# Loading the last 768 columns of one weight block as eight transfers of 21, 18, 10 and 1 rows

## The chip, the cores and the metric

The kernel runs on one core of one Trainium2 chip. The metric is device time in microseconds of that core, as the median of several executions. Most executions of one kernel agree within 0.3%; the trace holds the start, duration and size of every DMA packet and the moments at which the DMA engines that carry a transfer report their shares as landed. Neither record names the engine.

## The reference, cut to what matters

One token passes through grouped-query attention over a cache of 65536 keys and values in 4 groups, and beside it through a gated mixer. The two results are mixed with a gate. Only the last product of the attention half matters here:

```python
o = jnp.einsum('bhqk,bhkd->bhqd', p, v)
return o.transpose(0, 2, 1, 3).reshape(B, Sq, Hq * Dh) @ wo      # wo: 4096 x 1024, bf16, 8.4 MB
...
return g * a + (1 - g) * b
```

Everything is read once: 162 MB from HBM. So the time is that of one long load, with the arithmetic beside it.

## The kernel before

All large loads go through one queue, issued by the SP engine into a ring of buffers in SBUF. The order is fixed: keys and values, then the output weights as four quarters. Each quarter is 1024 rows of the matrix laid on 128 partitions, eight matrix rows (16 KB) a partition. The last quarter is cut in three, so that only a small piece is left for the end.

```python
def load(keys, src, off):
    n = len(stream)
    w = src.shape[1]
    ...
    stream.append((keys, off, src))

def rows(w, i, c):
    return w[128 * c * i:128 * c * (i + 1), :].rearrange("(p c) n -> p (c n)", c=c)
...
WO_AT = [0, 8 * DO, 16 * DO, 24 * DO]
WO_CUT = [(0, 5), (5, 7), (7, 8)]
for i in range(3):
    load([("wo", i, 0)], rows(A_wo, i, 8), WO_AT[i])
for c0, c1 in WO_CUT:
    load([("wo", 3, c0)], rows(A_wo, 3, 8)[:, DO * c0:DO * c1], WO_AT[3] + DO * c0)
...
P("SP", lambda e, o=OFF["RING"] + off, w=w, src=src: e.dma_start(arena[:, o:o + w], src),
  w=[("slot", x) for x in gr], dma="s%d" % gr[0])
```

A helper records each operation with what it reads and writes, and turns these into semaphore waits. It counts 16 on the semaphore for each complete transfer (`dma_count` in the kernel).

## Time and profile before

| | before |
|---|---|
| time, median | 381.83 us (381.75 to 382.3, 4 runs) |
| span in the profile | 380.3 us |
| data moved | 162.17 MB, 426 GB/s over the span |
| PE, DVE busy | 62%, 54% |
| latest landing of the last weights | 378.23 us |

The page has one row per engine or quantity over 40 slices of the span. The row of the transfer rate in the profile of the kernel before:

```profile
GB/s 435 427 420 400 469 388 438 441 469 431 401 414 441 441 443 427 434 410 424 477 441 434 434 434 414 415 441 441 434 407 433 445 441 441 436 403 424 419 426 262
```

Read it as a whole: with the DMA engines 90% busy or more in every slice but the last (the prediction shows that row), the rate stays around 430 GB/s. The prediction shows the other lines, and how the landings of single engines are read.

### The profile page before, as it was taken

Reading aid. Unit: us, or ns where it says so; the run is one execution under the profiler, and the core shown is the slowest. Engines: PE = TensorE matmul, PEld = TensorE weight load, DVE = VectorE, ACT = ScalarE, POOL = GpSimd, SP = SyncE. Lnnn points to the kernel's source line nnn. Section 1 sums busy time; section 2 is a strip of 40 time slices with the busy share of each in tenths; the row PEclk is TensorE's granted clock in tenths of the full one; section 3 lists DMA queues with packets and bytes.
Section 4 is the critical chain, followed back from the end, with each engine's and each line's share of the span. In section 5 each row is a group of like instructions: output and inputs, shape, how many; then the busy total and the mean of one; then the engine's idle time right before and its main releaser. Section 6 shows DMA issues by size and latency. Waiting matters only on the chain.

```text
span 380.3 us, 2581 instructions
## 1 busy us (share of the span) xinstructions
PE 235.1 (62%) x1449; PEld 58.1 (15%) x836; DVE 204.6 (54%) x162; ACT 23.3 (6%) x24; POOL 8.4 (2%) x37
## 2 busy tenths in 40 slices
PE   0061388458558924895788138952895884739378
PEld 0010011011111200122112001220121110212015
DVE  4011496778389525965892249745774882312020
ACT  1000000010420000002200000022000000220000
POOL 5000000000000000000000000000000000000000
PEclk9998599696859985998699859995899697958689
DMA  9999999999999999999999999999999999999996
GB/s 435 427 420 400 469 388 438 441 469 431 401 414 441 441 443 427 434 410 424 477 441 434 434 434 414 415 441 441 434 407 433 445 441 441 436 403 424 419 426 262
DMA packets 4254, 162.17 MB, mean 426 GB/s; under 512 B 532, under 2 KB 532, under 8 KB 788
## 3 DMA queue, kind: packets, MB, share of 16 engines
q1 hardware_dynamic: 4208, 162.01, 98.9%
q8 instruction: 9, 0.15, 0.2%
q10 hardware_dynamic: 36, 0.00, 0.0%
q14 instruction: 1, 0.01, 0.0%
HBM read 162.01 MB, written 0.00 MB: 426 GB/s over the span
## 4 chain that ended last, share of the span: by engine, by line
DMA 56%; PE 23%; DVE 18%; ACT 1%; issue 1%; SPq 0%; ACTq 0%; DVEq 0%
DMA arena<-in_A_k_cache_dram 34%; DVE arena L502 15%; DMA arena<-in_A_wo_dram 10%; DMA arena<-in_A_v_cache_dram 8%; PE scp L260 7%; PE scp L262 6%; DMA arena<-in_B_b_sp_dram 5%; PE obt L260 4%; PE obt L262 4%; DVE arena L539 1%; PE fbt L712 1%; PE fbt L660 1%; ACT arena L534 1%; SPq L389 0%; ACTq L288 0%
## 5 line engine op out<-in xcount | busy, mean ns | idle before, releaser
L502 DVE STREAM_TRANSPOSE arena<-arena 128x2048 f32<-128x2048 f32 x64 | 143.0, 2284 | 48.2 <-DMA arena<-in_A_k_cache_dram 32.7
L260 PE MATMUL scp<-arena 128*128 128x512 bf16 (+1 forms) x275 | 112.8, 429 | 87.7 <-DVE arena L502 86.3
L262 PE MATMUL scp<-arena 128*128 128x512 bf16 (+1 forms) x279 | 113.1, 427 | 0.0
L260 PE MATMUL obt<-arena 128*64 128x512 bf16 (+2 forms) x334 | 62.9, 419 | 17.5 <-DMA arena<-in_A_v_cache_dram 17.5
L262 PE MATMUL obt<-arena 128*64 128x512 bf16 (+2 forms) x334 | 62.2, 414 | 0.0
L260 PEld LDWEIGHTS scp<-arena 128*128 128x128 bf16 (+1 forms) x275 | 27.7, 104 | 200.1 <-issue 101.3
L539 DVE STREAM_TRANSPOSE arena<-arena 128x2048 bf16<-128x2048 bf16 x7 | 16.2, 2311 | 28.5 <-PE obt L262 26.4
L534 ACT ACTIVATE arena<-arena 128x2048 bf16<-128x2048 f32 x8 | 16.0, 2002 | 218.6 <-DVE arena L531 195.6
L260 PEld LDWEIGHTS obt<-arena 128*64 128x64 bf16 (+1 forms) x334 | 18.3, 113 | 70.7 <-issue 56.1
L519 DVE TENSOR_SCALAR_CACHE_REDUCE arena<-scp 128x2048 f32<-128x2048 f32 x8 | 18.3, 2292 | 16.0 <-PE scp L262 16.0
L580 PE MATMUL mbt<-arena 128*128 128x128 bf16 x16 | 1.9, 258 | 12.6 <-DVE arena L575 12.6
L542 DVE STREAM_TRANSPOSE arena<-arena 128x1024 bf16<-128x1024 bf16 x2 | 2.5, 1246 | 12.7 <-PE obt L262 12.7
L490 POOL COPY arena<-arena 32x32 bf16<-32x32 bf16 x16 | 3.2, 203 | 234.5 <-PE scp L262 209.7
L568 DVE RECIPROCAL arena<-mbt 128x1 f32<-128x1 f32 x4 | 0.6, 139 | 14.1 <-PE mbt L563 14.1
L531 DVE TENSOR_REDUCE arena<-mbt 128x1 f32<-128x32 f32 x4 | 0.8, 192 | 13.5 <-PE mbt L528 13.5
L437 PE MATMUL mbt<-arena 1*128 1x2 bf16 x1 | 0.2, 158 | 12.3 <-DMA arena<-in_B_b_sp_dram 12.3
L439 DVE COPY arena<-mbt 128x2 f32<-128x2 f32 x1 | 0.2, 160 | 12.3 <-PE mbt L437 12.3
L775 DVE CAST arena<-fbt 36x128 bf16<-36x128 f32 x1 | 0.3, 283 | 11.0 <-PE fbt L712 11.0
L432 PE MATMUL scp<-arena 8*128 8x1 bf16 x8 | 0.7, 199 | 8.7 <-DVE arena L427 8.7
L712 PE MATMUL fbt<-arena 128*32 128x128 bf16 x128 | 4.1, 220 | 0.1
L712 PEld LDWEIGHTS fbt<-arena 128*32 128x32 bf16 x128 | 3.6, 97 | 1.6 <-DMA arena<-in_A_wo_dram 0.8
L467 DVE CAST arena<-obt 97x1024 bf16<-97x1024 f32 x1 | 1.2, 1225 | 4.9 <-PE obt L262 4.9
(91 smaller groups left out, 54.2 us busy)
## 6 DMA issues: line engine op xcount, KB each, us to landing
arena<-in_A_k_cache_dram SPq DMA_DIRECT2D x6, 4096.0 KB, 33.1
arena<-in_A_v_cache_dram SPq DMA_DIRECT2D x2, 4096.0 KB, 26.0
arena<-in_B_w_in_dram SPq DMA_DIRECT2D x1, 7168.0 KB, 30.4
arena<-in_A_wo_dram SPq DMA_DIRECT2D x3, 2048.0 KB, 33.4
arena<-in_B_w_out_dram SPq DMA_DIRECT2D x1, 3584.0 KB, 21.5
arena<-in_A_wo_dram SPq DMA_DIRECT2D x1, 1280.0 KB, 30.3
arena<-in_A_wo_dram SPq DMA_DIRECT2D x1, 512.0 KB, 31.0
arena<-in_A_wo_dram SPq DMA_DIRECT2D x1, 256.0 KB, 30.8
```

The lines of the kernel that those rows point to most:

```text
L260: return e.matmul(*a, **kw)
L262: one = e.matmul(*a, **kw).ins
L467: P("DVE", lambda e: e.tensor_copy(psb[0:97, :], ob[0:97, :]), w=["psb", "ob"])
L490: P("POOL", lambda e, pb=pb: e.tensor_copy(vw(qpad, 24 + 32 * pb, [[QP, 4], [1, 8]], 32 * pb, 32), vw(qall, 8 * g, [[32, 4], [1, 8]], 32 * ...
L502: P("DVE", lambda e: e.transpose(ktb(i).bitcast(F32), sl[:, 4096 * p:4096 * (p + 1)].bitcast(F32)), r=keys[4 * p:4 * p + 4], w=[("kt", i % ...
L519: P("DVE", lambda e: e.tensor_scalar(scs(j), scp[:, :], 0.0, None, op0=ALU.add, op1=ALU.max, accum_out=maxc[:, j:j + 1]), w=[("sc", j % 2) ...
L534: P("ACT", lambda e: e.activation(psb2, scs(j), ACTF.Exp, bias=gcol(j // 2, K_NB), scale=SCALE, accum_out=lp[:, j:j + 1]), r=[("sc", j % 2 ...
L539: P("DVE", lambda e: e.transpose(ptsb2, psb2), r=["psb"], w=[("ptsb", 0), ("ptsb", 1)])
L542: P("DVE", lambda e: e.transpose(ptsb(n), ab("PSB", 1024, 1024 * (n % 2))), r=["psb"], w=[("ptsb", n % 2)])
L580: ins = e.matmul(mb[:, 0:128], sel[:, 128 * c:128 * (c + 1)], osc[:, 128 * c:128 * (c + 1)], start=(c == 0), stop=(c == 3))
L660: ins = e.matmul(fb[32 * b:32 * (b + 1), 0:QW], e4z[0:97, 31 - j:63 - j], part[0:97, QW * s:QW * (s + 1)], start=(first and s % (NW // 2) ...
L712: ins = e.matmul(fb[32 * b:32 * (b + 1), 0:QW], ovz[:, z:z + 32], sl[:, o:o + QW], start=False, stop=(i == 3 and c == 7), tile_position=(0 ...
```

## The change

Its intent: at the end of the load some DMA engines are done over a microsecond before others (seven of 16 landings of the last weights at 376.57 to 377.06 us, nine at 377.89 to 378.23). So a slice of one block, 768 of 8192 columns of the first quarter, is not shared equally among 16 engines but meant mainly for three of them. Each piece is written in the edit with the number of engines that it is meant for: 3, 9, 10 or 1.

```diff
-    def load(keys, src, off):
+    def load(keys, src, off, cut=None):
...
+        dst = arena[:, OFF["RING"] + off:OFF["RING"] + off + w]
+        parts = [(dst, src)]
+        if cut:
+            c, pieces = cut
+            parts = [(dst[:, 0:w - c], src[:, 0:w - c])]
+            for r0, step, k, h in pieces:
+                o, (row, _) = OFF["RING"] + off + w - c, src.ap[0]
+                parts.append((bass.AP(tensor=arena, offset=r0 * NA + o, ap=[[step * NA, h], [1, c]]),
+                              bass.AP(tensor=src.tensor, offset=src.offset + r0 * row + w - c,
+                                      ap=[[h // k * step * row, k], [step * row, h // k], [1, c]])))
...
+    LOW = [(r, 6, 3, 21) for r in (0, 2, 4)] + [(r, 6, 9, 18) for r in (1, 3, 5)] + [(109, 2, 10, 10), (126, 1, 1, 1)]
...
-        load([("wo", i, 0)], rows(A_wo, i, 8), WO_AT[i])
+        load([("wo", i, 0)], rows(A_wo, i, 8), WO_AT[i], cut=(768, LOW) if i == 0 else None)
...
-            P("SP", lambda e, o=OFF["RING"] + off, w=w, src=src: e.dma_start(arena[:, o:o + w], src),
-              w=[("slot", x) for x in gr], dma="s%d" % gr[0])
+            P("SP", lambda e, todo=todo: [e.dma_start(dst, x) for dst, x in todo],
+              w=[("slot", x) for x in gr], dma="s%d" % gr[0], parts=len(todo))
```

A piece (r0, step, k, h) takes h rows from r0 on, every step-th, and is meant for k engines.

More of the change, by code (lines that the diff above doesn't have):

```diff
@@ L29, in __init__, with op @@
         self.early = 0
-    def op(self, eng, fn, r=(), w=(), dma=None):
+    def op(self, eng, fn, r=(), w=(), dma=None, parts=1):
         o = Op()
@@ L50, in op @@
         if dma is not None:
-            self.dma_count[dma] = self.dma_count.get(dma, 0) + 16
+            self.dma_count[dma] = self.dma_count.get(dma, 0) + 16 * parts
             o.dma = (dma, self.dma_count[dma])
@@ L112, in run @@
                 if o.dma:
-                    last.then_inc(dsem[o.dma[0]], 16)
+                    for x in last if isinstance(last, list) else [last]:
+                        x.then_inc(dsem[o.dma[0]], 16)
                 elif o.inc:
@@ L312, in load @@
             place[key] = (n, off + i * (w // len(keys)), w // len(keys))
-        stream.append((keys, off, src))
+        dst = arena[:, OFF["RING"] + off:OFF["RING"] + off + w]
[8 more added lines that the diff above has]
+                                      ap=[[h // k * step * row, k], [step * row, h // k], [1, c]])))
+        stream.append((keys, off, w, parts))
     def rows(w, i, c):
@@ L379, in issue @@
             n = issued[0]
-            keys, off, src = stream[n]
-            w = src.shape[1]
+            keys, off, w, todo = stream[n]
             gr = grains(off, w)
```

## The prediction

> **What bounds the kernel now.** I read the page first, then busy time by stretches, the chain of waits, and last the timeline of the final microseconds. The page's rows by slice and its queue table say that the transfers fill the whole span:
>
> ```profile
> DMA  9999999999999999999999999999999999999996
> ...
> DMA packets 4254, 162.17 MB, mean 426 GB/s; under 512 B 532, under 2 KB 532, under 8 KB 788
> ...
> q1 hardware_dynamic: 4208, 162.01, 98.9%
> q8 instruction: 9, 0.15, 0.2%
> ```
>
> Every slice but the last is 90% busy or more, while PE is busy 62% of the span and DVE 54%. The stretches (columns: stretch, length, busy time of PE, PEld, DVE, ACT, POOL, then clock, DMA share, GB/s) show that only the first and last pieces have any slack:
>
> ```profile
> 60.00:180.00 120.00, 78.86 (x454) 18.36 (x242) 78.76 (x65) 10.30 (x11) 1.62 (x8) 0.83 1.00 433
> 180.00:300.00 120.00, 79.28 (x405) 17.50 (x208) 76.21 (x46) 6.28 (x6) 0.81 (x4) 0.83 1.01 435
> 360.00:376.50 16.50, 13.87 (x160) 5.23 (x121) 2.58 (x6) 1.02 (x1) 0.00 (x0) 0.84 0.98 414
> 376.50:380.30 3.80, 2.17 (x64) 1.79 (x64) 0.28 (x1) 0.00 (x0) 0.00 (x0) 1.00 0.19 69
> ```
>
> The chain in the last 12 us (start, length, what) goes through the output weights:
>
> ```profile
> 331.05 37.33 DMA arena<-in_A_wo_dram
> ...
> 376.50 1.77 PE fbt L712 x56
> ...
> 378.27 0.42 PE fbt L712 x8
> ```
>
> And the timeline shows the end: the last eight matmuls wait for the last piece of those weights, then a cast, then the store.
>
> ```profile
> 378.27 0.23 PEld L712 LDWEIGHTS fbt<-arena 128*32 128x32 bf16 x8 [0.18 <-DMA arena<-in_A_wo_dram]
> 378.79 0.28 DVE L775 CAST arena<-fbt 36x128 bf16<-36x128 f32 x1 [11.04 <-PE fbt L712]
> 379.10 0.31 SPq L366 DMA_DIRECT2D out_dram<-arena  x1
> ```
>
> The trace's semaphore marks give the 16 landings of that last piece: 376.57, .57, .60, .61, .65, .96, 377.06, then 377.89, .98, 378.03, .03, .12, .17, .18, .22, .23. So **seven engines end 1.2 to 1.7 us before the nine others**, and the kernel waits for 378.23. From there to the landing of the store at 380.27 is a fixed tail of 2.04 us. Time is therefore set by the slowest DMA engine. The mean of the 16 landings is 377.49, so perfect balance would be worth 0.74 us, 0.2% of the span: no larger gain is available.
>
> Why nine are late: the trace has nine fetches of 16 KB of instructions (55.3, 102.3, 133.6, 189.5, 245.2, 287.4, 329.6, 370.3 and 377.7 us; 0.97 to 1.10 us each) and one of 8 KB at 85.6. In the landings of each stage one more engine moves to the late group after each of these fetches. Data packets of one engine follow each other at a fixed few nanoseconds, so I followed packets back from each fetch. The first six 16 KB fetches lie on six engines that carry none of the eight-row load at the start; those of 329.6 and 370.3, and the 8 KB one, lead back to engines that do. The first placeholder store, also of eight rows, agrees: it lands at 376.11, .12, .15, .20, .63, 377.43, .56, .59, so three of its eight engines are late, and six of the other eight.
>
> [...] eight landings, against sixteen for 128 rows. Numbers it does not show. [...] A 64 KB row takes 2.418 us here, 27.1 GB/s[...].
>
> **The change part by part.** Removed: 768 of 8192 columns (1536 of 16384 bytes) in each of 128 rows of the first quarter, eight rows an engine. Added: the same bytes as 3 pieces of 21 rows on 3 engines (7 each), 3 of 18 on 9 (2 each), one of 10 on 10 and one of 1. Rows per engine: engine 0 gets 3x7+3x2+1+1 = 29, engines 1 and 2 get 28, engines 3 to 8 get 7, engine 9 gets 1, engines 10 to 15 none.
>
> Durations from the packet records: rows of 16384, 10240, 4096 and 2048 bytes take 614, 387, 159 and 84 ns, near 37 ns per 1024 bytes plus 8. So a 14848-byte row is about 557 ns (57 less) and a 1536-byte row about 65; a semaphore packet takes 9. Per engine:
> - engine 0: 29x65 + 8x9 - 8x57 = +1.50 us;
> - engines 1 and 2: 28x65 + 7x9 - 8x57 = +1.43 us;
> - engines 3 to 8: 7x65 + 4x9 - 8x57 = +0.04 us;
> - engine 9: -0.38; engines 10 to 15: -0.46 us.
>
> SP issues eight more transfers. Issues took 0.33 to 0.94 us, median 0.43; 8x0.43 = 3.4 us from 331 on, before its next wait, which ends at 345.7, and 30 us before the data: beside the path. PE's work is the same; it waits for the second quarter (landed 368.38) and the pieces after, so a later engine shifts all these waits and the end by the same amount. The end moves by the change of the latest landing.
>
> **Rivals.**
> (A) Engines 0 to 2 are all early. They go from 376.6 to 378.05; the upper late ones drop from 378.23 to 377.8; the three late ones below 8 stay. By the placeholder store's order these are the earliest of the late group, 377.9 to 378.03. End at 378.07: -0.15 us, 381.7. For it: the edit looks made for it, since +1.45 fills exactly the 1.45 us that the early ones have. Against it: nothing in the trace says that engines 0 to 2 are early.
> (B) Fetches walk upwards: six on 10 to 15, then 0 and 1. Then engines 0 and 1 are late already (377.9 to 378.03) and get 1.43 to 1.50 more: 379.4, +1.2 us, 383.1. For it: the order of six upper and then two lower ones, a consecutive walk being my assumption; the engine of 370.3 was the earliest of all until then, which is fully lost. Against: packets two nanoseconds apart cannot tell whether the seventh was on engine 0.
> (C) On top of either, [...] A with C is 376.6+3.0, so 379.6: +1.4 us, 383.3. B with C: about +2.8 us, 384.7. [...]
> (D) Eight issues block SP or the queue: no sign, with 30 us of queue; a stall of 10 us would be needed.
>
> **Range and chances.** Weights: A alone 0.23, B alone 0.27, A with C 0.22, B with C 0.28. Mean: 0.23x381.7 + 0.27x383.1 + 0.22x383.3 + 0.28x384.7 = 383.3; I take 383.1, the middle outcome. Low end 381.6 (A with run spread of 0.2), high end 384.8 (B with C). 2% is 7.6 us, ten times the most that balance can give and over twice the worst case: faster 0.01, same 0.97, slower 0.02.
>
> **What would show it.** The changed trace should have 128 rows of 1536 bytes, 14848-byte rows near 557 ns, and landings of the last piece in new groups. If A holds, the last landing is near 378.1 with a spread under 0.5 us among the latest twelve. If B, two landings stand alone about 1.3 us behind. If C, the 1536-byte packets take well over 65 ns. Wrong altogether if the tail after the last landing is not 2.04 us, if SP's next issue leaves 345.7, or if the fetches fall on other engines in the changed program.

It is read like this:

- "Engines 0 to 2" and the rows per engine are the assumption that a piece meant for k engines runs on k of them, always the same ones first. The trace gave counts only, eight landings for a load of eight rows and sixteen for one of 128. The packets counted below show 9, 10 and 1 engines for the pieces of 18, 10 and 1 rows, but seven for those of 21, and the landings of the markers are nested.
- The sums per engine, +1.50, +1.43 and +0.04 us, stand whole. Cut is the term of C, a cost of up to 57 ns more on each of 28 short rows, 1.6 us on engines 0 to 2, with no gain on the engines that lose rows; no trace showed it. With it A came to 376.6 + 3.0 = 379.6 us (time 383.3) and B to +2.8 us (384.7), and the weighted mean of the four to 383.3. Without it A has weight 0.45 and B 0.55, and the mean is 382.5.
- That one more engine is late after each fetch up to that of 370.3 us, in numbers: of the 16 landings of a block, those over 1.3 us behind the first are none in the block from 40.78 us, one from 57.74, two from 85.67 (after the 8 KB fetch), three from 105.02, four from 143.72, five from 201.85, six from 259.90, seven from 288.96, eight from 337.38 and nine in the last weights. The "few nanoseconds" are 3 or 4: so long before the end of a data packet start eight of the nine 16 KB fetches.

## The result, and the profile after

The changed kernel takes **383.0 us** (382.92 to 383.06, 4 runs) against 381.83 us. The ratio of the means is 1.0028, with a 95% interval of 1.0011 to 1.0045. Ratios in this document are the mean time of one kernel's runs over that of the other's in the same rounds, so they are not quite the ratio of the medians. The change is a loss of 1.2 us, within the 2% that counts as the same.

The page of the changed kernel, in the rows that the prediction and the section above showed of before:

```profile
DMA  9999989999999999999999999999989999999995
GB/s 440 440 426 398 440 386 436 440 488 437 435 426 419 392 435 440 440 422 436 441 433 440 440 433 440 435 440 440 433 378 424 457 440 440 435 409 426 398 406 240
DMA packets 4441, 162.17 MB, mean 425 GB/s; under 512 B 591, under 2 KB 719, under 8 KB 975
...
q1 hardware_dynamic: 4395, 162.01, 98.8%
q8 instruction: 9, 0.15, 0.2%
```

The engines are about as busy as before (two earlier slices fell below 90%), with the same bytes and the same nine instruction fetches. Single slices differ both ways in either run; in those that hold the changed loads, the 38th and 39th, the rate is 398 and 406 instead of 419 and 426 GB/s. Busy engines that move less is the first hint that this is not only a matter of balance.

**The packet counts show that the pieces did not run on the engines that the prediction names.** Each engine that carries a transfer ends its share with one packet of 4 bytes to the semaphore: the 128-row transfer of split16 (below) adds 16 such packets, the two transfers of cross64 add 32, and the markers on 1 to 15 engines add 120. Here queue q1 has 4395 - 4208 = 187 packets more than before: the 128 cut rows and 591 - 532 = 59 packets to semaphores. On 3, 9, 10 and 1 engines the eight pieces would have given 3x3 + 3x9 + 10 + 1 = 47. The count of 59 is 3x7 + 3x9 + 10 + 1: **the three pieces of 21 rows ran on seven engines each**. The source of such a piece is written as 3 groups of 7 rows, but with one stride throughout; why it ran on seven engines, the runs don't show. Rows per engine are then 17 on engine 0, 16 on each of 1 to 6, 7 on 7 and 8, 1 on engine 9 and none on 10 to 15, if the pieces use the engines in the order in which the markers below do. The prediction missed this; the sections below use the counted rows, taken as shared equally over the engines that a transfer's packets count (no record shows the shares).

The timeline of the last microseconds of the changed kernel answers to the one in the prediction (start, duration, engine, line, operation):

```profile
379.54 0.23 PEld L723 LDWEIGHTS fbt<-arena 128*32 128x32 bf16 x8 [0.20 <-DMA arena<-in_A_wo_dram]
380.06 0.28 DVE L786 CAST arena<-fbt 36x128 bf16<-36x128 f32 x1 [11.98 <-PE fbt L723]
380.37 0.31 SPq L378 DMA_DIRECT2D out_dram<-arena  x1
```

The three steps are the same, each 1.27 us later. The chain of waits of the changed kernel ends as before (start, length, what):

```profile
344.71 32.91 DMA arena<-in_A_wo_dram
...
377.75 1.76 PE fbt L723 x56
...
379.54 0.42 PE fbt L723 x8
```

It enters through the last quarter's pieces, and PE still waits for them. And the stretches show where the rate changed (columns as in the prediction):

```profile
60.00:180.00 120.00, 78.02 (x455) 18.21 (x242) 79.47 (x67) 10.43 (x12) 1.62 (x8) 0.85 1.00 432
180.00:300.00 120.00, 77.70 (x410) 17.27 (x210) 76.16 (x44) 6.15 (x6) 0.81 (x4) 0.87 1.01 434
360.00:376.50 16.50, 12.75 (x150) 4.84 (x116) 2.58 (x6) 1.02 (x1) 0.00 (x0) 0.82 1.00 397
```

Up to 300 us nothing has changed, 432 and 434 GB/s against 433 and 435. From 360 to 376.5 us it is 397 against 414. The 16 landings of the last piece of weights, from the semaphore records of the two traces (us, sorted):

```
before 376.57 .57 .60 .61 .65 .96 377.06 377.89 .98 378.03 .03 .12 .17 .18 .22 .23
after  377.14 .35 .50 .95 .96 378.10 .12 .17 .33 .38 .42 .59 .68 .92 379.45 .50
```

The latest landing moved from 378.23 to 379.50. The tail from there to the last landing of the store is 2.06 us (2.07 before, to 380.30; the prediction's 2.04 goes to the last landing but one, 380.27). What stands out is the mean of the landings: it went from 377.49 to 378.28. A mere exchange of work between engines would leave the mean almost where it was.

To compare runs closely I use one measure below, the **end stretch**: the mean of the 16 landings of the last weights, less the mean of the 16 landings of the last value block, which is queued just ahead of the cut quarter. It is 377.49 - 357.72 = 19.77 us before, and 378.28 - 357.69 = 20.60 us after. So each engine lost 0.83 us on average after the point where the change begins. The measure repeats well: the two kernels with markers that come below give 19.77 and 19.76 without the cut, and 20.61 and 20.58 with it.

The windows view of the three microseconds in which the cut pieces move (columns: stretch, length, busy time of PE, PEld, DVE, ACT, POOL, then granted clock, DMA share, GB/s), first before, then after:

```profile
361.00:364.00 3.00, 3.00 (x25) 0.74 (x11) 0.00 (x0) 0.00 (x0) 0.00 (x0) 0.83 1.01 431
```

```profile
361.00:364.00 3.00, 3.00 (x24) 0.72 (x10) 0.00 (x0) 0.00 (x0) 0.00 (x0) 0.74 1.10 352
```

The last two columns matter: the engines are fully busy in both (a share over 1 only means that packets are counted where they start), but the rate is 352 instead of 431 GB/s. In 3 us that is 0.24 MB less, which takes 0.55 us at 431 GB/s. So most of the 0.83 us seems to be lost right here (packets are counted where they start, so a stretch this short is rough).

The packet records name the packets that got longer (mean duration in ns; the smallest in brackets):

```
row bytes            before      after
14848 (first part)   -           582 (554), up to 812
1536 (cut pieces)    -           79 (65), up to 106
16384 (next rows)    616 (611)   646 (611), 45 of 256 over 700
10240, 4096, 2048    388 161 84  389 161 84
```

In the kernel before only one of the 16384-byte rows took over 700 ns (1159).

One more thing differs. SP's own timeline, before and then after:

```profile
347.03 0.37 SPq L366 DMA_DIRECT2D out_dram<-arena  x1
347.44 0.35 SPq L389 DMA_DIRECT2D arena<-in_A_wo_dram  x1
```

```profile
346.92 8.49 SPq L378 DMA_DIRECT2D out_dram<-arena  x1
355.45 1.57 SPq L400 DMA_DIRECT2D arena<-in_A_wo_dram  x1
```

With the eight added transfers SP is held for 8.49 us in the issue of the placeholder store (why, no record shows), and the last weights are issued at 355.45 instead of 347.44. They land more than 20 us later, behind what is queued, so this alone delays nothing.

### The profile page after: what moved, and what is told of

Read it like the earlier page. It is cut to its first block, busy times and chain, and to the rows that moved or that the text cites. A ratio compares the mean times of both kernels' runs of the same rounds, so it can differ in the third digit from the quotient of the medians.

```text
span 381.6 us, 2587 instructions
## 1 busy us (share of the span) xinstructions
PE 230.3 (60%) x1447; PEld 57.2 (15%) x836; DVE 204.1 (53%) x162; ACT 23.2 (6%) x24; POOL 9.4 (2%) x37
## 3 DMA queue, kind: packets, MB, share of 16 engines
q1 hardware_dynamic: 4395, 162.01, 98.8%
## 4 chain that ended last, share of the span: by engine, by line
DMA 57%; DVE 22%; PE 19%; ACT 1%; issue 1%; ACTq 0%; SPq 0%; DVEq 0%
DMA arena<-in_A_k_cache_dram 34%; DVE arena L513 18%; DMA arena<-in_A_v_cache_dram 10%; DMA arena<-in_A_wo_dram 9%; DMA arena<-in_B_b_sp_dram 5%; PE scp L261 5%; PE scp L263 5%; PE obt L261 4%; PE obt L263 3%; DVE arena L550 2%; PE fbt L723 1%; ACT arena L545 1%; ACTq L289 0%; PE fbt L671 0%; ACT arena L667 0%
## 5 line engine op out<-in xcount | busy, mean ns | idle before, releaser
L261 PE MATMUL scp<-arena 128*128 128x512 bf16 (+1 forms) x273 | 109.9, 424 | 89.4 <-DVE arena L513 86.6
L263 PE MATMUL scp<-arena 128*128 128x512 bf16 (+1 forms) x279 | 110.5, 420 | 0.5 <-issue 0.5
```

Source lines behind the costliest of these rows:

```text
L261: return e.matmul(*a, **kw)
L263: one = e.matmul(*a, **kw).ins
```

## The experiments

Two theories stood at the start, both with the prediction's wrong share of rows (28 or 29 on each of engines 0 to 2). **Theory 1** is the prediction's rival B: engines 0 and 1 are among the late ones, and the extra rows make late engines later. **Theory 2** is A with C: engines 0 to 2 are early, but the rows that are moved to them cost more than their bytes.

### First markers: probe_before and probe_after

The edit puts 15 tiny transfers of k = 1 to 15 rows behind the last weights, in both kernels. If marker k runs on the engines of marker k - 1 and on one more, the new landing of each marker names one engine, and engine k - 1 is the label of that one.

```diff
+            if issued[0] == len(stream):
+                for k in range(1, 16):
+                    P("SP", lambda e, k=k: e.dma_start(ab("SC", 16, 16 * k)[0:k, :], A_wo[0:k, 0:16]),
+                      w=[("prb", k)] + [("sc", 0)] * (k == 1), dma="prb%d" % k)
-        P("SP", ..., r=["orow"], w=["out"], dma="out")
+        P("SP", ..., r=[("prb", k) for k in range(1, 16)] + ["orow"], w=["out"], dma="out")
```

> The kernel before, with 15 marker transfers queued behind the last piece of weights: k rows of 32 bytes for k = 1 to 15[...]. Theory 1 (instruction fetches walk upwards over the engines): 0, 1 and 10 to 15 are late, near 378.0 to 378.3, one of 2 to 7 (the 8 KB fetch) is late too, 8 and 9 and the rest of 2 to 7 land near 376.6 to 377.1. Theory 2 (engines 0 to 2 are early[...]): 0, 1 and 2 land near 376.6. The span stays within 0.5 us of the kernel before.

> The changed kernel with the same markers. Theory 1: engines 0 and 1 are the two that stand alone at 379.45 and 379.50, engine 2 lands near 378, engines 10 to 15 near 377.5 to 378. Theory 2: engines 0, 1 and 2 all land together near 379.5, or the last ones are others than 0 and 1. The span stays within 0.5 us of the changed kernel, unless the issue queue stalls on the markers.

Both were a failure of construction. They took 386.57 and 388.15 us, with correct results. The markers waited for the placeholder store, which I had made a reader of the same names, and were issued only at 377.67 and 379.05 us, when the data was down. They name no engine. The two landing lists of the weights repeat those above within 0.31 us.

### Fewer instruction fetches: trim_before and trim_after

PE instructions were left out in both kernels (the result is wrong), all transfers kept, with the markers above.

```diff
-            for fe in range(4):
+            for fe in range(1 if p in (1, 2) else 4):
...
-                for b in range(2):
+                for b in range(1 if p in (1, 2) else 2):
...
-            for i in range(16):                                # value product
+            for i in [0, 1] + list(range(8, 16)):
```

> The kernel before with the markers and some 600 fewer PE instructions (score and value matmuls left out on purpose, the result is wrong), all transfers kept: some two and a half fewer 16 KB fetches before the end, so that engines 0 and 1 take none. Theory 1: six or seven late engines instead of nine, engines 0 and 1 land near 376.6, and the time stays within 0.3 us of the kernel before, as late upper engines still set it. Theory 2 says nothing of engines 0 and 1 and expects the same time too.

> The changed kernel with the same PE instructions left out (wrong result on purpose) and the markers. Theory 1: engines 0 and 1 start from 376.6 and take 1.5 to 1.9 us more for their 28 or 29 short rows (65 to 80 ns each), so they land at 378.1 to 378.5, and the loss of 1.2 us shrinks to between -0.2 and +0.3 us against the trimmed kernel before. Theory 2: the loss stays near 1.2 us, as it does not come from fetches.

The times are 388.9 and 391.4 us, ratios 1.017 and 1.0243 to the kernel before. Each contains the marker delay of the first try, and the trimmed kernel ran at a granted clock of 0.727 and reached the end stretch 2.4 us late (mean landing of the last value block 360.08 against 357.72), so the whole times say little (the expected time within 0.3 us of the kernel before was missed by 7 us). The end stretch is clean: 19.70 us without the cut, 20.44 with it, a loss of 0.74 us, and the latest landing moved by 1.30 us counted from the latest landing of the last value block. Fetches of 16 KB fell from nine to six:

```profile
q8 instruction: 6, 0.10, 0.1%
```

In the trimmed kernel before only four engines are clearly late (380.49 to 381.08; the other twelve land by 379.75). The loss from the cut is almost what it is with nine fetches, 0.74 against 0.83 us. Theory 1 spoke of the time, which goes with the latest landing: that loss should have shrunk to 0.3 us or less, and it is 1.30 us, against 1.19 us with nine fetches when counted in the same way. That speaks against theory 1.

### Markers again: mark_before and mark_after

The wait was removed and ten markers kept; only the last store reads them.

```diff
-                for k in range(1, 16):
+                for k in range(1, 11):
-        r=[("prb", k) for k in range(1, 16)] + ["orow"]
+        r=[("prb", k) for k in range(1, 11) if issued[0] == len(stream)] + ["orow"]
```

> The markers once more, mended: in the first try the markers waited for the placeholder store and were issued only at 377.7 us, after the data, so they named no engine. Now ten markers (k = 1 to 10) are queued behind the last weights without that wait, in the kernel before. Theory 1 (engines 0 and 1 are late by instruction fetches): the markers of k = 1 and 2 land near 378.0 to 378.1. Theory 2 (engines 0 to 2 early[...]): they land near 376.7. The span stays within 0.5 us of the kernel before.

> The changed kernel with the mended markers. Theory 1: engines 0 and 1 land last, near 379.5, having gained 1.5 us, and engine 2 near 378 to 378.5. Theory 2: engines 0 and 1, or 0 to 2, land near 379.5 too, but having gained 2.5 to 3 us against their markers in the kernel before. Engines 10 to 15: under theory 1 near 377.6 to 377.8; under theory 2 about where they were, 378.0 to 378.2.

They took 382.22 and 383.55 us (one run each, correct): 0.4 to 0.6 us more than the kernels without markers, so the markers themselves are seen but small. The first marker landing on each engine:

```
engine                       0      1      2      3      4      5      6      7      8      9
mark_before (us)          376.91 376.86 376.94 377.68 376.89 378.67 378.41 376.88 376.79 378.40
mark_after (us)           377.94 378.05 378.20 379.24 378.14 379.71 379.59 377.64 377.56 378.75
rise                       +1.03  +1.19  +1.26  +1.56  +1.25  +1.04  +1.18  +0.76  +0.77  +0.35
rows of the cut block      17     16     16     16     16     16     16      7      7      1
worked out               +0.72  +0.65  +0.65  +0.65  +0.65  +0.65  +0.65  +0.04  +0.04  -0.38
rest                     +0.31  +0.54  +0.61  +0.91  +0.60  +0.39  +0.53  +0.72  +0.73  +0.73
```

"Worked out" is the prediction's own sum with the rows that the packet counts give: 17x65 + 8x9 - 8x57 = +0.72 us for engine 0, 16x65 + 7x9 - 8x57 = +0.65 us for engines 1 to 6. "Rest" is the rise less that. (The last value block landed 0.15 us earlier in mark_after, so counted from there each rise is 0.15 us more.)

How one engine is read out of a marker: the landings are nested. Marker k has k of them, and on one engine successive markers land 0.17 to 0.22 us apart, so in the list of marker k every entry is the entry of marker k - 1 plus that step, and the one that is left over is engine k - 1. For k = 2 in the kernel before the two landings are 376.86 and 377.08; the second is engine 0's 376.91 plus 0.17, so 376.86 is engine 1.

This settles theory 1: **engines 0, 1 and 2 are early in the kernel before** (4, 7 and 8 too), and 5, 6, 9 and, by the remaining landings, five of 10 to 15 are late, with 3 in between. Theory 2's own forecast failed as well: engines 0 to 2 did not come near 379.5, and rose by 1.03 to 1.26 us instead of 2.5 to 3. The rises go in steps that fit the seven engines of the 21-row pieces: 1.03 to 1.56 us on engines 0 to 6, 0.76 and 0.77 on 7 and 8, 0.35 on 9. The two that set the end after the change are 5 and 6, late before and 1.04 and 1.18 us later now: about 0.65 us of it is the extra rows that the change gave them, and 0.39 and 0.53 us more is left over. That rest is there on every engine. Engines 10 to 15 lost all their 1536-byte rows, by the sum worth 8x57 ns = 0.46 us each, and gained nothing: the five late ones among them landed their last weights at 378.09 to 378.43 before and at 378.18 to 378.42 after. These are the entries that are left when the ten marked engines are taken out of the landing lists of the two runs; the sixth, early one is at 376.8 in both.

### The cut alone: split16

The same 768 columns were sent as one transfer of 128 rows over all 16 engines.

```diff
-            for r0, step, k, h in pieces:
-                ...
+            parts.append((dst[:, w - c:w], src[:, w - c:w]))
```

> The same 768 columns cut off, but sent as one transfer of 128 rows over all 16 engines, eight short rows each[...]. It pays for the second row packet and one more semaphore packet only: 8x(557+65-614)+9 = 73 ns more per engine. Both theories: last landing +0.1 us, ratio 1.000 to 1.001 against the kernel before; the short rows take 65 ns throughout[...].

The median is 382.07 us, ratio 1.0002 (0.9988 to 1.0016). The end stretch is 19.84 us, 0.07 more than before, as worked out. The short rows take 65 ns on average and at most 67, the 14848-byte rows 558. The windows view of split16:

```profile
361.00:364.00 3.00, 3.00 (x24) 0.80 (x10) 0.00 (x0) 0.00 (x0) 0.00 (x0) 0.73 1.05 434
```

The rate is 434 GB/s where the changed kernel had 352. So it is not the short rows and not the cut: it is how the rows are shared out, 17, 16, 7, 1 or none an engine instead of 8. The transfers are also eight instead of one; half, below, bears on that. The packet records then close the sum. Against split16, the change's 14848-byte rows are 582.0 - 558.2 = 23.8 ns longer, eight an engine (0.19 us); the short rows 79.4 - 65.3 = 14.1 ns, eight an engine on average (0.11 us); and the sixteen 16384-byte rows behind them 646.4 - 616.4 = 30.0 ns (0.48 us). Together that is 0.78 us, and the end stretches differ by 20.60 - 19.84 = 0.76 us.

### Equal shares, two transfers: cross64, with its control split4096

Here no engine is meant to get more or fewer bytes. 4096 of the 8192 columns go as two transfers of 64 rows (cross64) or as one of 128 rows (split4096).

```diff
-        load(..., cut=(768, LOW) if i == 0 else None)
+        load(..., cut=(4096, LOW) if i == 0 else None)
-            for r0, step, k, h in pieces:
-                ...
+            parts += [(dst[r0:r0 + 64, w - c:w], src[r0:r0 + 64, w - c:w]) for r0 in (0, 64)]   # cross64
+            parts.append((dst[:, w - c:w], src[:, w - c:w]))                                    # split4096
```

> The markers have refuted theory 1: engines 0 to 2 were early (376.67 to 376.75) and land near 377.8 to 378.0 after the change; the last ones are 5 and 6, which got no more bytes. [...] Test without any shift of load: 4096 of the 8192 columns go as two transfers of 64 rows, rows 0 to 63 and 64 to 127, eight rows of 8192 bytes an engine, so every engine has the bytes it had[...]. Theory 2: 8192-byte rows take up to 600 ns instead of about 310, and the last landing comes about 8x302 = 2.4 us later, time near 384.2 us, ratio 1.005 to 1.007. Rival (the loss comes from uneven shares, or from transfers on few engines): nothing but the split, +0.1 us, ratio 1.000.

> The control of cross64: the same 4096 columns as one transfer of 128 rows over 16 engines[...]. Theory 2: 8192-byte rows take about 309 ns throughout, and the mean landing of the last piece, counted from the mean landing of the last value block, stays at 19.77 us plus 0.05 (cross64: 23.19); ratio 1.000 to 1.001. Rival (a second transfer of long rows is what costs): over 1 us later, as in cross64.

The 8x302 ns = 2.4 us for cross64 is an estimate: it supposes that eight of an engine's 8192-byte rows take about as long again, 600 instead of 310 ns.

cross64 takes 385.94 us, ratio 1.0113 (1.0096 to 1.0129). split4096 takes 381.89 us, ratio 1.0000 (0.9982 to 1.0018); one run of the kernel before in its rounds took 599.71 us and is not used. The windows view, cross64 first, then split4096:

```profile
361.00:364.00 3.00, 3.00 (x24) 0.78 (x10) 0.00 (x0) 0.00 (x0) 0.00 (x0) 0.82 1.05 259
```

```profile
361.00:364.00 3.00, 3.00 (x22) 0.82 (x10) 0.00 (x0) 0.00 (x0) 0.00 (x0) 0.70 1.07 451
```

The engines are equally busy and the rate is 259 against 451 GB/s. The 8192-byte rows of cross64 (both halves of the cut quarter) take 459 ns on average and up to 635, in split4096 314 and at most 329. Each landing list shows 16 engines for each of the two transfers, so four rows of each on every engine if they are shared equally. Which rows an engine gets, and whether they are others than in one transfer of 128 rows, no record shows. The end stretch is 23.19 us against 19.84. Of these 3.35 us, 16 x (459 - 314) ns = 2.3 us are in those rows, near the 2.4 us that I expected, and 16 x (682 - 615) ns = 1.1 us are in the sixteen 16384-byte rows behind them, which I had left out; so the ratio came out above the expected 1.005 to 1.007. With equal shares a shift of load cannot explain this.

### Half the columns: half

```diff
-cut=(768, LOW)
+cut=(384, LOW)
```

> The change with 384 columns instead of 768, the same nine transfers and the same engines. Theory 2[...]: half the loss, +0.6 us, time near 382.4 us, ratio near 1.0015. Rival (the loss comes from nine transfers with their semaphores, and the 8.5 us stall of the issuing queue): the full +1.2 us, ratio near 1.003.

The median is 382.61 us (382.24 to 383.39), ratio 1.0024 (1.0009 to 1.0039). By time alone this decides nothing, since both 1.0015 and 1.003 are inside. The end stretch decides: 20.24 us, so a loss of 0.47 us for 384 columns against 0.83 us for 768. The number of transfers is the same, and SP is held by the same 8.49 us in the placeholder store. The latest landing, counted from the latest of the last value block, moved by 0.75 against 1.19 us. So most of the loss goes with the bytes and not with the number of transfers or the hold: a straight line through 0.47 and 0.83 us leaves 0.11 us for what doesn't. The windows view of half shows a rate between the other two:

```profile
361.00:364.00 3.00, 3.00 (x16) 0.84 (x8) 0.00 (x0) 0.00 (x0) 0.00 (x0) 0.50 1.04 376
```

### Rows in a row: contig

```diff
-    LOW = [(r, 6, 3, 21) for r in (0, 2, 4)] + [(r, 6, 9, 18) for r in (1, 3, 5)] + [(109, 2, 10, 10), (126, 1, 1, 1)]
+    LOW = [(r, 1, 3, 21) for r in (0, 21, 42)] + [(r, 1, 9, 18) for r in (63, 81, 99)] + [(117, 1, 10, 10), (127, 1, 1, 1)]
```

> The change with contiguous rows in each piece (rows 0 to 20, 21 to 41, 42 to 62 on three engines, and so on) instead of every sixth: the same rows per engine and the same engines. Theory 2: [...] the waits of the short rows are longer (mean over 80 ns) and single engines are delayed more unevenly; total loss 1.0 to 2.0 us. Rival (shares alone matter): the same time as the change within 0.2 us.

The median is 383.13 us, ratio 1.0037 (1.0022 to 1.0052); by time it can't be told from the change. The end stretch is 20.79 us, a loss of 1.02 instead of 0.83, and the short rows take 83 ns on average instead of 79. The latest landing of the weights is 380.32, alone at the end, with 379.62 next. So the stride of six in the change is worth about 0.2 us per engine, read from one profile of each; it softens the loss and does not remove it. (Its 21-row pieces ran on seven engines too: q1 has 4395 packets again. The expectation's three engines are the same mistake as in the prediction.) The stretches of contig:

```profile
361.00:364.00 3.00, 3.00 (x18) 0.71 (x8) 0.00 (x0) 0.00 (x0) 0.00 (x0) 0.50 1.06 328
```

## Why the prediction was right or wrong

**The bound and the tail: right.** The latest landing of the last weights sets the end. It moved by 1.27 us, and the tail stayed, 2.07 us before and 2.06 after.

**The price of the cut by itself: right.** Rows of 14848 and 1536 bytes were put at 557 and 65 ns; split16 has 558 and 65.3, and its end stretch grew by 0.07 us. ("Near 37 ns per 1024 bytes" is rounded down; the 557 ns needs 37.9, which is what the rows of 16384 and 2048 bytes give.)

**The engines of the pieces: wrong, and every rival rests on it.** The failed step is "3 pieces of 21 rows on 3 engines (7 each)". The prediction's check, eight landings for eight rows, did not cover a pattern of 3 groups of 7 rows. The 59 packets to semaphores put the 21-row pieces on seven engines, so "29" and "28" rows are 17 and 16, the sums of +1.50 and +1.43 us are +0.72 and +0.65, and engines 3 to 6 get +0.65 us instead of +0.04. What the change was meant to do, giving the rows to engines 0 to 2 (which are early), was never run, neither in the changed kernel nor in an experiment.

**Rival A: its premise right, its sum wrong.** Engines 0 to 2 are early, as the markers show. But the rows went also to 5 and 6, which were late, and to 3. Engines 0 to 2 landed at the marker times 377.94 to 378.20 and are not what sets the end, and the engines from 10 up did not come down by 0.46 us.

**Rival B: its engines wrong, its idea half right.** The failed step is "a consecutive walk being my assumption". Six of the upper engines are late, but the late ones below 8 are 5, 6 and, less, 3, not 0 and 1. That late engines get extra rows did happen, on 5 and 6 and with +0.65 us. The forecast for B, 383.1 us, is close to the 383.0 measured only by coincidence: it has 1.43 to 1.50 us of rows on two engines that were early, and no slower rows. The trimmed pair says of the fetches: with three fewer the loss is nearly as large. That fetches make engines late fits nine late engines with nine fetches (the 8 KB one and the eight of 16 KB up to 370.3 us) and, less closely, four with six, but no run tests it alone.

**Rival C: a cost beside the bytes right, its place wrong, its mechanism not shown.** C said that a moved short row costs up to 57 ns more, that this falls on engines 0 to 2 as 1.6 us, and that the unloaded engines gain nothing. The last part holds: 10 to 15 stayed where they were. The term that was mis-placed is the 1.6 us. The short rows became only 14 ns longer on average, and most of the loss lies in the long rows: 24 ns on each 14848-byte row and 30 ns on each 16384-byte row. The rest after each engine's own rows is 0.31 to 0.91 us on engines 0 to 9 and about 0.46 us on 10 to 15, not 1.6 us on three. As 5 and 6 were late already and got 16 short rows each, twice an equal share, they became the end. That the forecast for A with C fits too (383.3 us; its own terms give 383.2) is luck.

**The number.** 383.1 was a weighted middle of four sums, each with rows on the wrong engines, and 383.0 was measured. The mechanism behind the measured 1.2 us is another: about 0.65 us of extra rows on two late engines, an estimate from the measured durations, and the rest from rows that took longer.

**The 0.74 us to be had from balance: not had this way.** Two things are measured. Engines 10 to 15 lost their short rows, 0.46 us of work by the sum, and landed no earlier (the five late ones at 378.09 to 378.43 us before and 378.18 to 378.42 after). And the rate from 361 to 364 us fell from 431 to 352 GB/s with all engines busy. That two transfers of 64 rows cost rate against one of 128, with 16 engines on each, is shown by cross64 against split4096, 259 against 451 GB/s. What is shared there, in SBUF, on the side of HBM or elsewhere, no run shows: a packet record names neither engine nor partition.

**D, the issuing queue: half right.** SP was held by 8.49 us, close to the 10 us that I estimated would be needed for harm (345.7 us less the end of the issues at 331 + 3.4 us is 11 us), and the eight issues took 5.9 us (330.87 to 336.76) instead of 3.4. It did no visible harm: half has the same hold and about half the loss, and cross64 has no hold (0.38 us) and the largest loss. The sign "SP's next issue leaves 345.7" did come, it went out at 344.34, but it waits for PE and its data is due 20 us later.

**Still open.** The rest after the own rows differs from engine to engine, from 0.31 us on engine 0 to 0.91 on engine 3, by one marked run of each kernel. Single engines can't be followed through the pieces in the trace, so why is not known. How the 1.2 us of the end divides into own rows and longer rows is worked out and not measured: no run gives the rows to early engines alone.

No version that beats the kernel before came out of this. Every variant here in which the cut columns went otherwise than as one transfer of 128 rows was slower, by 0.24% to 1.1%; none gave the extra rows to early engines alone.

## What to carry to other kernels

When all DMA engines are busy from the start to the end, look at the rate beside the busy share: here fully busy engines moved 352 GB/s instead of 431 while the cut pieces ran. Unequal landings at the end do not by themselves mean that work can be moved; in this kernel sharing out 768 columns in this way cost each engine 0.83 us on average. Count the packets to semaphores to see on how many engines a transfer ran, before any sum is built on it: 59 instead of 47 would have corrected this one. Tiny marker transfers on 1, 2, 3, ... engines behind the last load are a cheap way (ten of them took 0.4 to 0.6 us here) of learning which engine is late, before a change is built on a guess.
